# Transposes of v moved from DMA to TensorE, squared norms of k moved off it, gate bias preset in both tail banks, all ranks redrawn: a scheduled attention and highway kernel

## Chip, cores and metric

The kernel runs on one core of one Trainium2 chip. The metric is the device time of one execution in microseconds. A program on one core has no die to compare, so a run counts as fast unless it is over 1.5% above the fastest of its kernel. Ratios and their intervals are from fast runs alone. In the profile lines, PE is TensorE, PEld its weight loads, DVE VectorE, ACT ScalarE, POOL GpSimd and SP SyncE; L800 is line 800 of the kernel.

## The reference, cut to what matters

```python
# q, k, v: (4, 6336, 256) float32; tau = 1
qn = q / (np.linalg.norm(q, axis=1, keepdims=True) + 1e-06)    # norms over the 6336 rows
kn = k / (np.linalg.norm(k, axis=1, keepdims=True) + 1e-06)
s = kn.transpose(0, 2, 1) @ qn / tau                           # 256 x 256 for each batch
a = softmax(s)                                                 # over the last axis
x = (v @ a).reshape(-1, 256)                                   # 25344 x 256
H = np.maximum(x @ w_h, 0.0)
T = 1.0 / (1.0 + np.exp(-(x @ w_t + b_t)))
out = T * H + (1.0 - T) * x
```

## The kernel before

Each of the four batches has two stages. **Stage 1** runs over 50 subtiles of q and k (48 of 128 rows, two of 96) and adds up k'q, and beside it k'k and q'q, of which only the diagonals (the squared norms) are used. Then comes the **softmax chain**: norms, scaling, exp, and the folding of the two weight matrices into the attention matrix. **Stage 2** runs over 25 pairs of subtiles of v: v is transposed, and three products give h (before relu), t (before the gate) and x; ScalarE does relu and tanh, VectorE combines. Stage 1 of batch b+1 is woven into stage 2 of batch b. The 100 pairs are numbered through; "the tail" is what comes after pair TAIL, where stage 1 is over and its two PSUM banks serve h and t.

All of this goes through a planner: every piece of work is a task with an engine, a key (its rank: a smaller key goes first), durations, buffers that it takes and gives back. The planner simulates the engines and emits instructions in the order that it found. The constants at the top are ranks by kind of work, one number for each of batches 0, 1, 2 (from 2 on) and for the tail, and the order of loads.

```python
UNTIL = 73; AHEAD = 16; BY_DMA = 3; APART = 5; V_AHEAD = 2     # one line each in the file
PRIO = {
    ...
    "bias": (-28.394, 23.065, -1.772, 4.453),                  # batch 0, 1, 2, tail
    ...
}
HEAD = 5.5
TAIL = 66
ENDS = [18, 48.5, 62.25]        # pairs at which stage 1 of batches 1, 2, 3 is to be loaded

def stage1(b, s):               # cut
    for c in range(2):
        nc.tensor.matmul(sg[c][:, 0:C], kc, qa, start=first, stop=False)
        nc.tensor.matmul(sg[c][:, C : C + P], kc, kc, start=False, stop=False)
        if not apart(b, s // CH):            # b > 0 and chunk < APART: squares of q elsewhere
            nc.tensor.matmul(sg[c][:, C + P : C + 2 * P], qa[:, cs], qa[:, cs], ...)

def squares(b, j, half): ...    # ScalarE: Square of half a q chunk, 128 x 1024
def sum_squares(b, j, step): ...# GpSimd: adds them up to 128 x 256
def over_partitions(): ...      # TensorE: four small 32-bit matmuls against ones
# VectorE then adds that to the diagonal, and the softmax chain goes on

def transposes(b, i):           # TensorE; batch 3 as 16-bit, the others two halves as one 32-bit
def transpose_chunk(b, j):      # batch 3, chunks 3 to 6, by DMA on the queue of the stores
    nc.sync.dma_start(out=..., in_=src, transpose=True)

def preset(b, i):               # gate bias copied into the bank ahead of the products
    return t_tag(b, i) == "t"   # else a 512-column matmul row0 x btb puts it there
```

## Time and profile before

| | before |
|---|---|
| time, median of 4 runs | 269.76 us (269.4 to 270.33) |
| span of the profiled run | 268.3 us |
| first product of stage 2, last matmul, end | 45.65, 262.36, 268.35 us |
| TensorE work between these two, at full rate | 210.17 us |
| gaps of TensorE between these two | 6.65 us |

"Work" and "gaps" are used all through this text. Work is the sum over matmuls of the start-to-start distance at full rate (0.109 us for 256 columns and for a 32-bit transpose, 0.056 for 128, 0.216 for 512; the prediction shows how the timeline gives them). A gap is what lies between two starts beyond that. So the span is the first product (45.65) plus work plus gaps plus the end, less 0.11 us of the last matmul, which is in both the work and the end; the two sums are computed from the starts in the trace, and no matmul record is missing. Gaps before 90 us differ by up to about 1 us between runs with the same order there (1.5 to 2.3 us), so less than that is not read as an effect.

The groups of TensorE work that the change touches, in the list of groups by line and form; columns: line, engine, operation, tiles, shapes, count, then busy us and mean ns, then idle time before:

```profile
L453 PE MATMUL sg<-k 128*128 128x128 f16 x384 | 76.8, 223 | 0.0
L455 PE MATMUL sg<-q 128*128 128x128 f16 x144 | 32.5, 226 | 0.0
L760 PE MATMUL vtps<-ident,v 128*128 128x128 f32 x144 | 27.8, 275 | 0.9 <-DMA v<-in_v_dram 0.6 <-ACT vtsb L533 0.3
L754 PE MATMUL vtps<-ident,v 128*128 128x128 f16 x48 | 4.6, 219 | 0.0
L831 PE MATMUL t<-btb,row 128*128 128x512 f16 x16 | 6.1, 379 | 0.0
```

The counts matter here, not the busy times, in which pipelined matmuls overlap.

### The profile page before, as it was taken

Reading aid. Unit: us, or ns where it says so; the run is one execution under the profiler, and the core shown is the slowest. Engines: PE = TensorE matmul, PEld = TensorE weight load, DVE = VectorE, ACT = ScalarE, POOL = GpSimd, SP = SyncE. Lnnn points to the kernel's source line nnn. Section 1 sums busy time; section 2 is a strip of 40 time slices with the busy share of each in tenths; the row PEclk is TensorE's granted clock in tenths of the full one; section 3 lists DMA queues with packets and bytes.
Section 4 is the critical chain, followed back from the end, with each engine's and each line's share of the span. In section 5 each row is a group of like instructions: output and inputs, shape, how many; then the busy total and the mean of one; then the engine's idle time right before and its main releaser. Section 6 shows DMA issues by size and latency. Waiting matters only on the chain.

```text
span 268.3 us, 6249 instructions
## 1 busy us (share of the span) xinstructions
PE 246.4 (92%) x2430; PEld 216.6 (81%) x2430; DVE 181.6 (68%) x377; ACT 195.1 (73%) x365; POOL 131.7 (49%) x167
## 2 busy tenths in 40 slices
PE   0697977999999999999999999999999999999991
PEld 0596864889989978999999878999998778888880
DVE  1000035777766789557878797586878998998994
ACT  1001016978888789999898887787798999998980
POOL 7233468688778064695689138567655110000000
PEclk9999999999999999999999999999999999999998
DMA  6999999999999999999999999999999999999995
GB/s 107 215 211 208 206 206 202 212 213 214 214 213 212 213 214 255 247 263 269 275 286 258 267 267 254 249 236 281 287 280 239 284 214 304 379 399 165 351 423 232
DMA packets 24622, 67.24 MB, mean 251 GB/s; under 512 B 9104, under 2 KB 11280, under 8 KB 21648
## 3 DMA queue, kind: packets, MB, share of 16 engines
q0 software_dynamic: 13472, 39.20, 75.0%
q1 hardware_dynamic: 11120, 27.64, 29.0%
q8 instruction: 19, 0.31, 0.4%
q14 instruction: 11, 0.09, 0.1%
HBM read 78.38 MB, written 25.95 MB: 389 GB/s over the span
## 4 chain that ended last, share of the span: by engine, by line
PE 76%; DMA 12%; ACT 5%; POOL 2%; issue 2%; DVE 2%; ACTq 0%; DVEq 0%; POOLq 0%
PE h L800 16%; PE t L800 16%; PE d L800 15%; PE sg L452 12%; DMA k<-in_k_dram 10%; PE sg L453 6%; PE vtps L760 5%; DMA v<-in_v_dram 2%; ACT uu L854 2%; PE sg L455 2%; PE t L831 1%; PE vtps L754 1%; PE ah L689 1%; POOL q L327 1%; ACT d L840 1%
## 5 line engine op out<-in xcount | busy, mean ns | idle before, releaser
L800 PEld LDWEIGHTS <-vtsb 128*128 128x128 f16 (+1 forms) x1044 | 98.8, 99 | 17.3 <-issue 3.2
L452 PE MATMUL sg<-q,k 128*128 128x256 f16 x384 | 83.8, 277 | 12.7 <-DMA k<-in_k_dram 12.6
L861 DVE SCALAR_TENSOR_TENSOR pp<-uu,d 128x512 f32<-128x512 f32 (+1 forms) x100 | 68.0, 684 | 28.4 <-PE d L800 16.1
L453 PE MATMUL sg<-k 128*128 128x128 f16 x384 | 76.8, 223 | 0.0
L854 ACT ACTIVATE uu<-t 128x512 f32<-128x512 f32 (+1 forms) x100 | 59.7, 597 | 19.1 <-PE t L800 18.5
L880 DVE SCALAR_TENSOR_TENSOR o<-h,pp 128x512 f32<-128x512 f32 x96 | 65.5, 686 | 1.7
L840 ACT ACTIVATE d<-h 128x512 f32<-128x512 f32 (+1 forms) x100 | 57.9, 584 | 5.7 <-PE h L800 4.9
L800 PE MATMUL t<-mr,vtsb 128*128 128x256 f16 (+1 forms) x348 | 52.2, 272 | 1.5 <-ACT t L533 1.2
L800 PE MATMUL h<-mr,vtsb 128*128 128x256 f16 (+1 forms) x348 | 51.2, 272 | 0.5 <-ACT vtsb L533 0.5
L800 PE MATMUL d<-mr,vtsb 128*128 128x256 f16 (+1 forms) x348 | 51.5, 272 | 0.1
L452 PEld LDWEIGHTS <-k 128*128 128x128 f16 x384 | 38.0, 99 | 16.7 <-DMA k<-in_k_dram 13.9
L476 POOL TENSOR_TENSOR sq<-sq,sq 128x1024 f32<-128x1024 f32 x15 | 35.4, 2361 | 16.7 <-ACT sq L470 16.6
L453 PEld LDWEIGHTS <-k 128*128 128x128 f16 x384 | 38.0, 99 | 1.5
L533 ACT COPY t<-bias_all 128x512 f32<-128x512 f32 (+1 forms) x60 | 35.4, 591 | 1.4
L455 PE MATMUL sg<-q 128*128 128x128 f16 x144 | 32.5, 226 | 0.0
L470 ACT ACTIVATE sq<-q 128x1024 f32<-128x1024 f16 x30 | 31.3, 1053 | 0.0
L760 PE MATMUL vtps<-ident,v 128*128 128x128 f32 x144 | 27.8, 275 | 0.9 <-DMA v<-in_v_dram 0.6
L569 DVE SCALAR_TENSOR_TENSOR junk<-sg,ident 128x128 f32<-128x128 f32 x16 | 4.6, 288 | 33.2 <-PE sg L455 32.7
L535 DVE COPY vtsb<-vtps 128x256 f32<-128x256 f32 (+2 forms) x47 | 19.6, 418 | 7.0 <-PE vtps L760 6.7
L327 POOL DMA_DIRECT2D v<-in_v_dram x24 | 13.7, 571 | 18.9 <-PE vtps L760 11.7
L327 POOL DMA_DIRECT2D q<-in_q_dram x28 | 15.4, 552 | 15.1 <-DMA q<-in_q_dram 7.1
L327 POOL DMA_DIRECT2D k<-in_k_dram x28 | 15.3, 548 | 13.1 <-DMA k<-in_k_dram 9.2
(78 smaller groups left out, 249.5 us busy)
## 6 DMA issues: line engine op xcount, KB each, us to landing
out_dram<-o SPq DMA_DIRECT2D x23, 1024.0 KB, 9.6
v<-in_v_dram POOLq DMA_DIRECT2D x24, 512.0 KB, 16.6
q<-in_q_dram POOLq DMA_DIRECT2D x21, 512.0 KB, 16.2
k<-in_k_dram POOLq DMA_DIRECT2D x21, 512.0 KB, 18.0
q<-in_q_dram POOLq DMA_DIRECT2D x5, 256.0 KB, 9.6
k<-in_k_dram POOLq DMA_DIRECT2D x5, 256.0 KB, 8.9
out_dram<-o SPq DMA_DIRECT2D x2, 512.0 KB, 4.2
out_dram<-ot SPq DMA_DIRECT2D x4, 192.0 KB, 5.1
```

Source lines behind the costliest of these rows:

```text
L327: nc.gpsimd.dma_start(out=t[:, s : s + n, :], in_=main_rows(src)[:, j * CH + s : j * CH + s + n, :])
L452: nc.tensor.matmul(sg[c][:, 0:C], kc, qa, start=first, stop=False)
L453: nc.tensor.matmul(sg[c][:, C : C + P], kc, kc, start=False, stop=False)
L455: nc.tensor.matmul(sg[c][:, C + P : C + 2 * P], qa[:, cs], qa[:, cs], start=False, stop=last)
L476: add(out=sq, in0=sq, in1=other)
L533: nc.scalar.copy(out=out, in_=in_)
L760: nc.tensor.transpose(ps[:, u, 0:nr], v.bitcast(f32), ident0[0:nr, 0:nr])
L800: nc.tensor.matmul(out[0:nr, u, :], vt[u][kt][:, 0:nr], mr[kt][:, col * C : (col + 1) * C], **flags(u, kt))
L840: nc.scalar.activation(out=d[0:nr, :, :], in_=ps_t["h", b, i][0:nr, :, :], func=Act.Relu, scale=0.5)
L854: nc.scalar.activation(out=uu[0:nr, :, :], in_=ps_t.pop(("t", b, i))[0:nr, :, :], func=Act.Tanh, scale=-0.5)
L861: nc.vector.scalar_tensor_tensor(out=pp[0:nr, :, :], in0=el.pop(("uu", b, i))[0:nr, :, :], scalar=1.0, in1=ps_t.pop(("d", b, i))[0:nr, :, ...
L880: nc.vector.scalar_tensor_tensor(out=ot, in0=ps_t.pop(("h", b, i))[0:nr, :, :], scalar=0.0, in1=el.pop(("pp", b, i))[0:nr, :, :], op0=AluO ...
```

## The change

The intent is threefold: no DMA transposes (they slow other transfers), fewer matmuls for squared norms (two k chunks a batch, with one q chunk a batch given back), and fewer bias matmuls in the tail (ScalarE or VectorE copies the bias into either bank for three pairs in four). All ranks and the order of loads were drawn again.

```diff
-UNTIL = 73
-AHEAD = 16
-BY_DMA = 3
+UNTIL = 61
+AHEAD = -15                    # without effect: nothing is transposed by DMA
+BY_DMA = 7
-APART = 5
-V_AHEAD = 2
+APART = 4
+APART_K = 2
+V_AHEAD = 0.5
 PRIO = {
-    "bias": (-28.394, 23.065, -1.772, 4.453),
+    "bias": (-15.797, -52.319, -73.352, 56.321),
     ...                        # all other rows redrawn as well
 }
-HEAD = 5.5
-TAIL = 66
-ENDS = [18, 48.5, 62.25]
+HEAD = 8.5
+EVERY = 4
+TAIL = 64
+ENDS = [22.5, 42.25, 58.5]
...
-        return b == B - 1
+        return b == B - 1 and BY_DMA <= NJ          # natural(b): never now
...
-            nc.tensor.matmul(sg[c][:, C : C + P], kc, kc, start=False, stop=False)
-            if not apart(b, s // CH):
+            if not apart("k", b, s // CH):
+                nc.tensor.matmul(sg[c][:, C : C + P], kc, kc, start=False, stop=False)
+            if not apart("q", b, s // CH):
...                             # squares, sum_squares, plan_squares: for q and for k
-        return t_tag(b, i) == "t"
+        return t_tag(b, i) == "t" or (b * NP + i) % EVERY != 1
...
-                        lambda e, i=i: bias(b, i, e), take=["t"],
+                        lambda e, i=i: bias(b, i, e), take=[t_bank],
```

More of the change, by code (lines that the diff above doesn't have):

```diff
@@ L21 @@
 LAG = 5
-UNTIL = 73
-AHEAD = 16
-BY_DMA = 3
+UNTIL = 61
+AHEAD = -15
+BY_DMA = 7
 SHORT = 1.08
 MOVE = 165e3
-APART = 5
-V_AHEAD = 2
+APART = 4
+APART_K = 2
+V_AHEAD = 0.5
 PRIO = {
-    "tr": (24.974, 16.445, 34.195, 63.304),
-    "ev": (74.59, 73.008, 67.512, 50.704),
-    "h": (-53.39, -86.015, -64.208, -14.641),
-    "bias": (-28.394, 23.065, -1.772, 4.453),
-    "t": (4.111, -1.918, 67.766, 74.312),
-    "relu": (46.555, -20.175, -1.498, 14.915),
-    "x": (0.958, -19.433, 43.343, -6.4),
-    "gate": (-54.132, 37.28, -94.231, -112.222),
-    "prod": (-40.861, -10.819, -26.763, -55.482),
-    "res": (53.604, 18.42, 116.457, -9.113),
-    "s1": (117.419, 42.459, 84.45),
-    "sq": (-15.195, 72.384, 19.395),
+    "tr": (-41.544, -84.484, -71.287, -73.219),
+    "ev": (79.702, 164.382, 118.864, 152.575),
+    "h": (-104.744, -35.547, 40.328, 54.671),
+    "bias": (-15.797, -52.319, -73.352, 56.321),
+    "t": (-63.659, -149.979, -3.104, -73.919),
+    "relu": (-161.99, -110.892, 56.133, -126.746),
+    "x": (-150.758, -174.281, -305.464, -51.983),
+    "gate": (-109.784, -55.547, -191.652, -71.681),
+    "prod": (125.206, 114.192, 152.224, 33.14),
+    "res": (12.493, 105.005, -95.23, -167.161),
+    "s1": (78.544, 189.464, 249.341),
+    "sq": (-44.364, -12.223, -5.305),
 }
 POW = 0.75
-HEAD = 5.5
-TAIL = 66
+HEAD = 8.5
+EVERY = 4
+TAIL = 64
 EV = BIAS = ("ACT", "DVE")
-ENDS = [18, 48.5, 62.25]
+ENDS = [22.5, 42.25, 58.5]
 class Ring:
@@ L266 @@
         "q": QK_BUFS, "k": QK_BUFS, "v": V_BUFS, "tail_q": 2, "tail_k": 2, "tail_v": 2,
-        "sq": 2, "vT": 3, "vT_t": 1, "o": O_BUFS, "ot": 1, "uu": 3, "pp": 3, "vtsb": 9, "mr0": 2, "mr1": 2,
+        "sqq": 2, "sqk": 2, "vT": 3, "vT_t": 1, "o": O_BUFS, "ot": 1, "uu": 3, "pp": 3, "vtsb": 9, "mr0": 2, "mr1": 2,
         "sg0": 1, "sg1": 1, "vt": 1, "t": 1, "h": 2, "d": 2,
@@ L457, in stage1, with apart, squares, sum_squares @@
                 )
-    def apart(b, j):
-        return b > 0 and j < APART
+    def apart(nm, b, j):
+        return b > 0 and j < {"q": APART, "k": APART_K}[nm]
     sq_t = {}
     sums = {}
-    def squares(b, j, half):
-        sq_t[b, j, half] = sq = new("sq", [P, CH // 2, C], f32, f"sq{b}_{j}_{half}")
-        qa = tiles[("q", b, j)][:, half * CH // 2 : (half + 1) * CH // 2, :]
-        nc.scalar.activation(out=sq, in_=qa, func=Act.Square)
-    def sum_squares(b, j, step):
+    def squares(nm, b, j, half):
+        sq_t[nm, b, j, half] = sq = new("sq" + nm, [P, CH // 2, C], f32, f"sq{nm}{b}_{j}_{half}")
+        x = tiles[(nm, b, j)][:, half * CH // 2 : (half + 1) * CH // 2, :]
+        nc.scalar.activation(out=sq, in_=x, func=Act.Square)
+    def sum_squares(nm, b, j, step):
         add = partial(nc.gpsimd.tensor_tensor, op=AluOp.add)
         if step == 0:
-            sq, other = sq_t[b, j, 0], sq_t.pop((b, j, 1))
+            sq, other = sq_t[nm, b, j, 0], sq_t.pop((nm, b, j, 1))
             add(out=sq, in0=sq, in1=other)
         elif step == 1:
-            sq = sq_t[b, j, 0]
+            sq = sq_t[nm, b, j, 0]
             add(out=sq[:, 0:2, :], in0=sq[:, 0:2, :], in1=sq[:, 2:4, :])
         else:
-            sq = sq_t.pop((b, j, 0))
+            sq = sq_t.pop((nm, b, j, 0))
             if j == 0:
-                sums[b] = small.tile([P, C], f32, tag="sums", name=f"sums{b}")
-                add(out=sums[b], in0=sq[:, 0, :], in1=sq[:, 1, :])
+                sums[nm, b] = small.tile([P, C], f32, tag=f"sums{nm}", name=f"sums{nm}{b}")
+                add(out=sums[nm, b], in0=sq[:, 0, :], in1=sq[:, 1, :])
             else:
                 add(out=sq[:, 0, :], in0=sq[:, 0, :], in1=sq[:, 1, :])
-                add(out=sums[b], in0=sums[b], in1=sq[:, 0, :])
-    def plan_squares(b):
+                add(out=sums[nm, b], in0=sums[nm, b], in1=sq[:, 0, :])
+    def plan_squares(nm, b):
         ends, x = {}, None
-        for j in range(APART):
-            key = slot_of((b - 1) * NS + CH * j) + PRIO["sq"][b - 1]
+        for j in range({"q": APART, "k": APART_K}[nm]):
+            key = slot_of((b - 1) * NS + CH * j) + PRIO["sq"][b - 1] + (nm == "k")
             n0 = len(plan.tasks)
@@ L496, in plan_squares @@
                 plan.add(
-                    "ACT", key, 0.97, 1.07, loaded("q", b, CH * j + CH // 2 * n),
-                    lambda j=j, n=n: squares(b, j, n), take=["sq"],
+                    "ACT", key, 0.97, 1.07, loaded(nm, b, CH * j + CH // 2 * n),
+                    lambda j=j, n=n: squares(nm, b, j, n), take=["sq" + nm],
                 )
@@ L503, in plan_squares @@
             y = plan.add(
-                "POOL", key, 2.36, 2.45, parts, lambda j=j: sum_squares(b, j, 0), drop=[(parts[1], "sq")]
+                "POOL", key, 2.36, 2.45, parts, lambda j=j: sum_squares(nm, b, j, 0), drop=[(parts[1], "sq" + nm)]
             )
-            y = plan.add("POOL", key, 1.27, 1.35, [y], lambda j=j: sum_squares(b, j, 1))
+            y = plan.add("POOL", key, 1.27, 1.35, [y], lambda j=j: sum_squares(nm, b, j, 1))
             x = plan.add(
                 "POOL", key, 1.3 if j else 0.65, 1.4 if j else 0.75, [y] + ([x] if x else []),
-                lambda j=j: sum_squares(b, j, 2), drop=[(parts[0], "sq")],
+                lambda j=j: sum_squares(nm, b, j, 2), drop=[(parts[0], "sq" + nm)],
             )
@@ L513, in over_partitions @@
         def over_partitions():
-            sums[b, "ps"] = ps = new("vt", [P, 2], f32, f"sumps{b}")
+            sums[nm, b, "ps"] = ps = new("vt", [P, 2], f32, f"sumps{nm}{b}")
             for c in range(2):
-                nc.tensor.matmul(
-                    ps[:, c : c + 1], sums[b][:, bass.ts(c, P)], ones[:, 0:1], start=c == 0, stop=c == 1
-                )
+                x = sums[nm, b]
+                if nm == "q" or natural(b):
+                    x = x[:, bass.ts(c, P)]
+                else:
+                    x = x.rearrange("p (w two) -> p two w", two=2)[:, c, :]
+                nc.tensor.matmul(ps[:, c : c + 1], x, ones[:, 0:1], start=c == 0, stop=c == 1)
         def keep():
-            sums[b, "sb"] = sb = small.tile([P, 2], f32, tag="sumsb", name=f"sumsb{b}")
-            nc.vector.tensor_copy(out=sb, in_=sums[b, "ps"])
+            sums[nm, b, "sb"] = sb = small.tile([P, 2], f32, tag=f"sumsb{nm}", name=f"sumsb{nm}{b}")
+            nc.vector.tensor_copy(out=sb, in_=sums[nm, b, "ps"])
         p = plan.add("PE", key + 2, 0.4, 0.6, [x], over_partitions, take=["vt"])
@@ L535, in copy, with plan_chain @@
             nc.vector.tensor_copy(out=out, in_=in_)
-    def plan_chain(b, own, last, key, sums_of_q):
+    def plan_chain(b, own, last, key, apart_sums):
         st = {}
@@ L601, in dcat, with rest_of @@
                 )
-        def rest_of_q():
-            if sums_of_q:
-                xq = st["x"][:, 0:2]
-                nc.vector.tensor_tensor(out=xq, in0=xq, in1=sums[b, "sb"], op=AluOp.add)
+        def rest_of(nm, n):
+            if b:
+                x = st["x"][:, n : n + 2]
+                nc.vector.tensor_tensor(out=x, in0=x, in1=sums[nm, b, "sb"], op=AluOp.add)
         dq = dve(
-            lambda: (diagonal(0), diagonal(1), rest_of_q()), 0.9, 0.95, [last, consts] + sums_of_q
+            lambda: (diagonal(0), diagonal(1), rest_of("q", 0)), 0.9, 0.95, [last, consts] + apart_sums[:1]
         )
         nq = pool(lambda: norm(0), POW, POW + 0.2, [dq])
-        dk = dve(lambda: (diagonal(2), diagonal(3)), 0.75, 0.8, [dq])
+        dk = dve(
+            lambda: (diagonal(2), diagonal(3), rest_of("k", 2)), 0.9 if b else 0.75, 0.95 if b else 0.8,
+            [dq] + apart_sums[1:],
+        )
         nk = pool(lambda: norm(2), POW, POW + 0.2, [dk])
@@ L819, in preset @@
     def preset(b, i):
-        return t_tag(b, i) == "t"
+        return t_tag(b, i) == "t" or (b * NP + i) % EVERY != 1
     def bias(b, i, e):
         nr = rows(2 * i)
-        ps_t["t", b, i] = t = new("t", [P, 2, C], f32, f"t{b}_{i}")
+        ps_t["t", b, i] = t = new(t_tag(b, i), [P, 2, C], f32, f"t{b}_{i}")
         copy(e, t[0:nr, :, :], bias_all[0:nr, :, :])
@@ L937, in plan_stage1 @@
         x, own = None, []
-        part_ends, sums_of_q = ({}, []) if not apart(b, 0) else plan_squares(b)
+        part_ends, apart_sums = {"q": {}, "k": {}}, []
+        if b:
+            for nm in "qk":
+                part_ends[nm], z = plan_squares(nm, b)
+                apart_sums.append(z)
         for n, s in enumerate(order_of(b)):
@@ L941, in plan_stage1 @@
             deps = loaded("q", b, s) + loaded("k", b, s) + ([x] if x else [])
+            away = [nm for nm in "qk" if apart(nm, b, s // CH)]
             x = plan.add(
-                "PE", key, 0.33 if apart(b, s // CH) else 0.44, 0.66, deps, lambda s=s: stage1(b, s),
+                "PE", key, 0.44 - 0.11 * len(away), 0.66, deps, lambda s=s: stage1(b, s),
                 take=[sg_tag(b, n)] if n < 2 else [],
-                drop=([] if apart(b, s // CH) else drops("q", b, s)) + drops("k", b, s),
+                drop=[z for nm in "qk" if nm not in away for z in drops(nm, b, s)],
             )
             x.lat = x.pitch if n < NS - 1 else 0.66
-            if apart(b, s // CH) and s % CH == CH - 1:
-                plan.add("NONE", 0, 0, 0, [x] + part_ends[s // CH], None, drop=drops("q", b, s))
+            if s % CH == CH - 1:
+                for nm in away:
+                    plan.add("NONE", 0, 0, 0, [x] + part_ends[nm][s // CH], None, drop=drops(nm, b, s))
             if n < 2:
                 own.append((x, sg_tag(b, n)))
-        ready[b] = plan_chain(b, own, x, -50, [sums_of_q] if apart(b, 0) else [])
+        ready[b] = plan_chain(b, own, x, -50, apart_sums)
         if b == B - 1:
@@ L999, in plan_stage2 @@
                     plan.add(
-                        BIAS, pr("bias", g), (0.5, 0.6), (0.63, 0.72), [b_all] + before,
-                        lambda e, i=i: bias(b, i, e), take=["t"],
+                        BIAS, pr("bias", g), (0.5, 0.6), (0.63, 0.72), [b_all] + before + ends_of[t_bank],
+                        lambda e, i=i: bias(b, i, e), take=[t_bank],
                     )
```

## The prediction

> **What bounds the kernel now.** I read the page first (busy shares, slices, chain that ended last), then busy time by ten-microsecond stretch, then the timeline, because the pitch of instructions is only visible there.
>
> ```profile
> PE 246.4 (92%) x2430; PEld 216.6 (81%) x2430; DVE 181.6 (68%) x377; ACT 195.1 (73%) x365; POOL 131.7 (49%) x167
> PE   0697977999999999999999999999999999999991
> DMA  6999999999999999999999999999999999999995
> HBM read 78.38 MB, written 25.95 MB: 389 GB/s over the span
> PE 76%; DMA 12%; ACT 5%; POOL 2%; issue 2%; DVE 2%; ACTq 0%; DVEq 0%; POOLq 0%
> ```
>
> TensorE is busy in every slice from about 50 us on, and the chain of waits runs over TensorE for 76% of the span. But the DMA row is as full, so both are candidates. By stretch:
>
> ```profile
> 40.00:50.00 10.00, 8.19 (x67) 5.84 (x66) 6.18 (x15) 7.31 (x15) 8.62 (x11) 1.00 1.10 205
> 150.00:160.00 10.00, 9.07 (x91) 7.92 (x88) 8.48 (x30) 7.97 (x20) 3.01 (x5) 1.00 1.06 265
> 230.00:240.00 10.00, 9.99 (x100) 8.60 (x98) 9.54 (x16) 8.96 (x18) 0.00 (x0) 1.00 1.02 412
> 240.00:250.00 10.00, 10.00 (x92) 8.60 (x90) 9.20 (x16) 9.19 (x18) 0.00 (x0) 1.00 1.17 220
> ```
>
> Columns: stretch, length, then busy us of PE, weight load, VectorE, ScalarE, GpSimd, granted clock, DMA share, GB/s. In 240 to 250 us the DMA share is highest (1.17) while the rate falls from 412 to 220 GB/s: that is where v chunks of the last batch are transposed by DMA. TensorE does not go idle for it. VectorE and ScalarE are at 9.0 to 9.5 of 10 in the tail.
>
> "Busy" is not "at peak", so I took start-to-start distances from the timeline:
>
> ```profile
> 226.58 0.60 PE L800 MATMUL h<-mr,vtsb 128*128 128x256 f16 x4
> 227.01 0.60 PE L800 MATMUL d<-mr,vtsb 128*128 128x256 f16 x4
> 227.45 0.39 PE L754 MATMUL vtps<-ident,v 128*128 128x128 f16 x4
> 227.68 0.60 PE L800 MATMUL t<-mr,vtsb 128*128 128x256 f16 x4
> ...
> 248.71 0.38 PE L831 MATMUL t<-btb,row 128*128 128x512 f16 x1
> 248.93 0.27 PE L800 MATMUL t<-mr,vT 128*128 128x256 f16 x1
> ```
>
> Four 256-column products take 0.437 us (226.58 to 227.01 to 227.45), so 0.109 each; four 16-bit transposes 0.23; a 512-column bias matmul 0.22 (248.71 to 248.93). Two 32-bit transposes also take 0.22 (121.91 to 122.13 in the timeline). A whole subtile half of stage 1 (one 256- and two 128-column matmuls) repeats every 0.22 us (87.54 to 87.76), so a 128-column matmul is 0.055. Multiplying these by the counts of each line in each stretch gives work at full rate: 9.9 to 10.2 us in nearly every ten-microsecond stretch from 60 to 260. So TensorE really is the bound there. The exceptions are 50 to 60 (9.7), 90 to 100 (9.3), 150 to 160 (8.8) and 200 to 220 (19.1 of 20.4): the stretches where the softmax chain of the next batch runs. Gaps in all: about **5 us**. Stage 2 starts at 45.65 us; before that DMA bounds (batch 0's q and k must land, then the first v chunk, which lands at 44.6). After the last matmul (262.6) some 6 us of VectorE, store and landing remain.
>
> **What the Trainium skill says.** "TensorE: Matmul & The Clock Gate", section "Wait — 56ns, not 53.3ns?", gives start-to-start 55.6 ns for 128 columns and 215.7 ns for 512 once warm; the trace agrees (0.055 and 0.22 us), at a granted clock of 1.00. "Perfetto Trace Analysis", section "Identifying the Most-Contended Engine", warns that matmul busy time is no measure of distance to the roofline; hence the pitches above. "ScalarE: Activation LUTs", section "What ACT_TABLE_LOAD costs", says an ACTIVATE with immediates takes 186 ns + 0.833 ns per element and back-to-back ones overlap by about 93 ns. For 512 elements that is 613 and 520; the trace has 0.59 and 0.49 to 0.50:
>
> ```profile
> 225.47 0.59 ACT L854 ACTIVATE uu<-t 128x512 f32<-128x512 f32 x1
> 225.95 0.59 ACT L840 ACTIVATE d<-h 128x512 f32<-128x512 f32 x1
> 226.47 0.58 ACT L533 COPY t<-bias_all 128x512 f32<-128x512 f32 x1
> 226.97 0.60 ACT L854 ACTIVATE uu<-t 128x512 f32<-128x512 f32 x1
> ```
>
> So busy times of ScalarE are counted at 0.5 us per 512-wide instruction below. "Advanced Engine Details and Errata", section "X-Bar Transpose (TRN2)", calls transpose DMAs as fast as regular ones; the 220 against 412 GB/s above does not look like it.
>
> **The change part by part, on TensorE.**
> 1. No v transposed by DMA. Three chunks (12 pairs) and the short tail pair of the last batch, 13 pairs, now take two 32-bit transposes each: 13 x 0.22 = **+2.9 us**. The other 12 pairs of that batch swap four 16-bit for two 32-bit ones: 0.23 for 0.22, nothing.
> 2. k's squares of two chunks a batch leave TensorE: 3 batches x 16 subtiles x 2 = 96 matmuls x 0.055 = **-5.3**. But the eight subtiles of batch 1's first chunk run at 38.3 to 42.4 us, where TensorE is waiting anyway: 16 x 0.055 = 0.9 of that buys nothing.
> 3. The diff also lowers APART from 5 to 4: one q chunk a batch returns: 3 x 8 x 2 = 48 x 0.055 = **+2.6**.
> 4. k's sums over partitions need four more small matmuls a batch, 0.36 to 0.44 us before the next instruction (85.79 to 86.23, 204.94 to 205.30): 3 x 0.4 = **+1.2**.
> 5. Bias matmuls: odd pairs after pair 66 (17) become pairs with remainder 1 by four after pair 64 (65, 69, ... 97: 9): 8 x 0.22 = **-1.8**.
>
> Sum: 2.9 - 5.3 + 2.6 + 1.2 - 1.8 = -0.4; after 45.65 us, where it counts, -0.4 + 0.9 = **+0.5 us**. Thus the changed operations are nearly a trade of TensorE work against itself.
>
> **On the other engines.** ScalarE gains three net chunks of squares (2 x 3 x about 1.0 us = +6) and GpSimd about three adding-ups of 2.4 + 1.3 + 1.5 = 5.2 (+15). Bias presets rise by 8 (+4 to 5 us on either engine). v evictions become 25 narrow ones in place of 12 wide (25 x about 0.32 - 8 x 0.5 - 4 x 0.35 = +2.6). Body stretches have room. For the tail I count per pair: TensorE 3 x 0.437 + 0.22 + 0.22/4 = 1.59; ScalarE 2 x 0.5 + 0.29 eviction + 0.75 x 0.5 = 1.67 (0.29 is an estimate from 0.374 less the overlap), VectorE 2 x 0.61 = 1.22; shared evenly that is about 1.46 each. TensorE stays the bound, but with ScalarE and VectorE at 92%, which leaves little for bad order. Before, the DMA-transposed pairs took only 1.31 + 0.11 = 1.42 on TensorE.
>
> **On DMA.** The transposes go. At 220 instead of about 400 GB/s for ten microseconds they cost at least 4.5 us of DMA capacity; with the other two perhaps 6 to 10 (estimate). As TensorE did not wait for it, this by itself buys nothing. It makes room for the rest of the diff: q and k of the last batch are asked for some four pairs earlier (ENDS 62.25 to 58.5), stores are let loose at pair 61 rather than 73.
>
> **Retuned order.** All priorities are redrawn. What they can win is the 5 us of gaps around the chains and some idle time between 36.7 and 45.65 us; the latter hangs on landings that keep their order. I expect the tuner to have found about half of the gaps, -2.5 us, since someone kept this version. That is a choice, not a working.
>
> **Rivals.** (a) *Nothing is won*: the gaps stay, the +0.5 counts, and the time is 270 to 271. For it: gaps come from the chain itself, whose steps are unchanged. (b) *ScalarE and VectorE become the bound of the tail*: with a preset in each bank, each bank waits copy, products, tanh in a row (0.6 + 0.6 + 0.6 us), and with 92% load every hiccup shows. 33 pairs x 0.1 = 3 us more: 272 to 273. For it: tail stretches already at 9.0 to 9.5 of 10. Against: those count overlapping spans; at true pitch 8 to 10% is free. (c) *GpSimd delays loads*: four adding-ups in the first two chunks of a batch, about 20 us of in-order work, on the engine that issues loads. If a load is late, TensorE starves: +1 to 3 us. Against: 51% idle. (d) *DMA was the hidden limit*: total traffic 104.3 MB at the 420 GB/s of 10 to 40 us (210 GB/s counted on the 16-bit side, twice that read) is 248 us, plus start and transposes about 263, close to the span. If stores or late v throttle the pairs indirectly, removing 6 to 10 us lets TensorE close its gaps: 264 to 266. Against: no DMA wait of TensorE after 50 us among the longest waits.
>
> **Range and chances.** 269.9 + 0.5 - 2.5 = **267.9 us**. Rivals (a) to (c) reach 271.2 at moderate weight; (d) or a very good order reaches 265.2: range 265.2 to 271.2. Faster by over 2% needs under 264.5, i.e. all the gaps and more: 0.08. Slower by over 2% needs above 275.3, several rivals at once: 0.05. Within 2%: 0.87.
>
> **What would show it.** TensorE: 200-odd 32-bit transposes and none by DMA, 9 bias matmuls, 288 instead of 384 full k-square matmuls, 192 instead of 144 full q ones, work at full rate after 45 us within 1 us of before. DMA share near 240 us falls and GB/s no longer dips. Tail per pair near 1.59 us; if it is 1.7 or more with TensorE waiting for ScalarE or VectorE, (b) is right. Gaps near 95, 155 and 205 to 220 us should be about half. Wrong would be: a start of stage 2 well off 45.6 us, TensorE waiting for landings after 50 us, or a body that shortens by more than its work.

## More of the kernel before

The DMA part of the page:

```profile
DMA packets 24622, 67.24 MB, mean 251 GB/s; under 512 B 9104, under 2 KB 11280, under 8 KB 21648
q1 hardware_dynamic: 11120, 27.64, 29.0%
```

Queue q1 carries stores and DMA transposes.

## The result, and the profile after

| | before | after |
|---|---|---|
| time, median of 4 runs | 269.76 us | 271.17 us (270.89 to 271.3) |
| ratio | | 1.0041, 95% interval 1.0019 to 1.0062 |
| span of the profiled run | 268.35 | 269.04 |
| first product of stage 2 | 45.65 | 45.50 |
| work from there to the last matmul | 210.17 | 210.75 |
| gaps | 6.65 | 7.94 |
| of these before 90, 90 to 198, after 198 us | 1.6, 2.9, 2.1 | 1.5, 3.3, 3.2 |
| last matmul to end | 5.99 | 4.96 |

The change is slower by 0.4%: within 2%, but on the other side of zero than foretold. In the profiled runs, which lie 0.69 us apart: -0.15 (start) +0.58 (work) +1.29 (gaps) -1.03 (end) = +0.69.

The page after, the lines that answer to those of the prediction:

```profile
PE 246.1 (91%) x2388; PEld 216.8 (81%) x2388; DVE 191.7 (71%) x409; ACT 200.3 (74%) x366; POOL 143.9 (53%) x176
PE   0697977999999998999999899999999999999992
DMA  6999999999999999999999999999999999974435
HBM read 78.38 MB, written 25.95 MB: 388 GB/s over the span
PE 63%; DMA 20%; DVE 6%; POOL 4%; ACT 3%; issue 3%; DVEq 0%; POOLq 0%; ACTq 0%
```

The DMA row drops to 3 to 5 tenths in the last slices: the capacity is free. TensorE does not profit. That the chain has 20% DMA where it had 12% is no new bound: 8.6% of the span is one load, of the last rows of v of batch 1, which took 23.1 us, and TensorE waits 0.2 us for it. The groups of the changed work, by line and form, have the counts that were foretold (288 and 192 squares, 192 whole 32-bit transposes, 9 bias matmuls):

```profile
L456 PE MATMUL sg<-k 128*128 128x128 f16 x288 | 61.1, 224 | 0.0
L458 PE MATMUL sg<-q 128*128 128x128 f16 x192 | 42.9, 224 | 0.0
L770 PE MATMUL vtps<-ident,v 128*128 128x128 f32 x192 | 36.9, 274 | 0.7 <-DMA v<-in_v_dram 0.7
L841 PE MATMUL t<-btb,row 128*128 128x512 f16 x9 | 3.4, 379 | 0.0
```

And the DMA part of the page:

```profile
DMA packets 17869, 65.56 MB, mean 244 GB/s; under 512 B 2352, under 2 KB 4528, under 8 KB 14896
q1 hardware_dynamic: 4368, 25.96, 24.0%
```

Without the transposes there are 6752 fewer packets under 512 bytes. Stretches of ten microseconds after (columns as in the prediction):

```profile
150.00:160.00 10.00, 9.23 (x79) 7.62 (x76) 9.41 (x29) 8.42 (x20) 6.94 (x11) 1.00 1.06 276
210.00:220.00 10.00, 9.33 (x77) 7.48 (x76) 8.93 (x20) 8.97 (x20) 0.12 (x1) 1.00 1.03 327
230.00:240.00 10.00, 10.00 (x92) 8.90 (x91) 9.89 (x20) 9.23 (x18) 0.00 (x0) 1.00 0.93 312
240.00:250.00 10.00, 10.00 (x94) 9.02 (x92) 9.78 (x20) 9.55 (x19) 0.00 (x0) 1.00 0.53 215
```

VectorE is now at 9.8 to 9.9 in the tail, and still TensorE has no gaps there: between 225 and 262 us they sum to nothing (before: 0.7 us). The gaps stand where they stood, around the last two chains, and the one of the last batch is larger: 2.4 us between 198 and 225 us, where it was 1.4. The stretch of the kernel before that answers to the second line above:

```profile
210.00:220.00 10.00, 9.85 (x79) 7.67 (x77) 9.36 (x21) 9.48 (x23) 0.53 (x1) 1.00 1.07 247
```

Of the 2.4 us, 1.0 lies in two gaps at 215.2 and 216.3 us, where TensorE waits for ScalarE to write the folded matrix of the last batch; the kernel before has no such wait there.

The shorter end comes from the last store. The last VectorE result and the last issue before,

```profile
263.89 0.69 DVE L880 SCALAR_TENSOR_TENSOR ot<-h,pp 96x512 f32<-96x512 f32 x1
264.60 0.33 SPq L892 DMA_DIRECT2D out_dram<-ot  x1
```

and after:

```profile
265.25 0.69 DVE L890 SCALAR_TENSOR_TENSOR ot<-h,pp 96x512 f32<-96x512 f32 x1
265.96 0.33 SPq L902 DMA_DIRECT2D out_dram<-ot  x1
```

From issue to the end of the span it is 3.75 us before (268.35) and 3.08 after (269.04). The DMA engines are less busy by then (share 0.30 between 250 and 260 us, before 1.02); that this is what shortens it is not shown.

### The profile page after: what moved, and what is told of

It is laid out like the page before. It is cut to its first block, busy times and chain, and to the rows that moved or that the text cites. A ratio compares the mean times of both kernels' runs of the same rounds, so it can differ in the third digit from the quotient of the medians.

```text
span 269.0 us, 6180 instructions
## 1 busy us (share of the span) xinstructions
PE 246.1 (91%) x2388; PEld 216.8 (81%) x2388; DVE 191.7 (71%) x409; ACT 200.3 (74%) x366; POOL 143.9 (53%) x176
## 4 chain that ended last, share of the span: by engine, by line
PE 63%; DMA 20%; DVE 6%; POOL 4%; ACT 3%; issue 3%; DVEq 0%; POOLq 0%; ACTq 0%
PE h L810 13%; PE d L810 13%; PE t L810 13%; DMA k<-in_k_dram 10%; PE sg L454 9%; DMA v_t<-in_v_dram 9%; PE vtps L770 6%; PE sg L456 4%; DVE pp L871 2%; DMA v<-in_v_dram 2%; PE sg L458 2%; DVE o L890 2%; POOL q L329 1%; POOL k L329 1%; DVE vtsb L542 1%
## 5 line engine op out<-in xcount | busy, mean ns | idle before, releaser
L810 PEld LDWEIGHTS <-vtsb 128*128 128x128 f16 (+1 forms) x1200 | 114.6, 99 | 19.2 <-issue 5.2
L454 PE MATMUL sg<-q,k 128*128 128x256 f16 x384 | 80.3, 277 | 13.8 <-DMA k<-in_k_dram 12.9
L871 DVE SCALAR_TENSOR_TENSOR pp<-uu,d 128x512 f32<-128x512 f32 (+1 forms) x100 | 68.1, 682 | 19.2 <-PE d L810 14.9
L864 ACT ACTIVATE uu<-t 128x512 f32<-128x512 f32 (+1 forms) x100 | 59.5, 596 | 13.8 <-PE t L810 12.1
L456 PE MATMUL sg<-k 128*128 128x128 f16 x288 | 61.1, 224 | 0.0
L454 PEld LDWEIGHTS <-k 128*128 128x128 f16 x384 | 38.1, 100 | 18.1 <-DMA k<-in_k_dram 14.1
L458 PE MATMUL sg<-q 128*128 128x128 f16 x192 | 42.9, 224 | 0.0
L770 PE MATMUL vtps<-ident,v 128*128 128x128 f32 x192 | 36.9, 274 | 0.7 <-DMA v<-in_v_dram 0.7
L479 POOL TENSOR_TENSOR sqq<-sqq,sqq 128x1024 f32<-128x1024 f32 x12 | 28.4, 2369 | 8.7 <-ACT sqq L473 8.6
L542 DVE COPY vtsb<-vtps 128x256 f32<-128x256 f32 x70 | 29.2, 418 | 3.8 <-PE vtps L770 2.9
L456 PEld LDWEIGHTS <-k 128*128 128x128 f16 x288 | 28.7, 100 | 1.0
L770 PEld LDWEIGHTS vtps<-ident,v 128*128 128x128 f32 x192 | 23.4, 141 | 3.1 <-PE ah L699 1.1
L473 ACT ACTIVATE sqq<-q 128x1024 f32<-128x1024 f16 x24 | 25.0, 1052 | 0.0
L542 DVE COPY t<-bias_all 128x512 f32<-128x512 f32 x26 | 18.0, 692 | 9.1 <-ACT uu L864 8.9
```

Of the source, the lines that this page charges most:

```text
L479: add(out=sq, in0=sq, in1=other)
L542: nc.vector.tensor_copy(out=out, in_=in_)
L770: nc.tensor.transpose(ps[:, u, 0:nr], v.bitcast(f32), ident0[0:nr, 0:nr])
L810: nc.tensor.matmul(out[0:nr, u, :], vt[u][kt][:, 0:nr], mr[kt][:, col * C : (col + 1) * C], **flags(u, kt))
L864: nc.scalar.activation(out=uu[0:nr, :, :], in_=ps_t.pop(("t", b, i))[0:nr, :, :], func=Act.Tanh, scale=-0.5)
L871: nc.vector.scalar_tensor_tensor(out=pp[0:nr, :, :], in0=el.pop(("uu", b, i))[0:nr, :, :], scalar=1.0, in1=ps_t.pop(("d", b, i))[0:nr, :, ...
```

## The experiments

Twelve kernels ran, each beside the kernel before on the same chip (its medians there: 270.2 to 270.4 us), and all gave right results. All parts are planned, so a change of one constant can move thousands of instructions; some mixtures could not be planned at all ("no task can start": buffers held in a circle), and one raced. In old_parts_new_loads one of the six runs (299.42 us) is slow by the rule above and is not in the ratio; all other runs are fast. The table has the results; work, gaps and end are of the profiled runs.

| run | time us | ratio to before | work | gaps | of these after 198 us | end |
|---|---|---|---|---|---|---|
| before | 269.8 | 1 | 210.17 | 6.65 | 2.1 | 6.0 |
| after | 271.2 | 1.004 | 210.75 | 7.94 | 3.2 | 5.0 |
| old_no_dma_transpose | 272.8 | 1.008 | 212.94 | 6.56 | 1.8 | 5.4 |
| old_nodma_preset | 276.4 | 1.022 | 211.00 | 12.75 | 7.6 | 5.3 |
| nodma_preset_rank | 272.6 | 1.009 | 211.00 | 8.99 | 3.7 | 5.4 |
| old_k_squares | 275.2 | 1.018 | 209.70 | 11.52 | 4.0 | 6.3 |
| k_squares_rank | 279.8 | 1.034 | 209.70 | 16.04 | 7.6 | 6.6 |
| new_parts_old_order | 286.3 | 1.058 | 210.53 | 22.25 | 14.8 | 5.8 |
| old_parts_new_priorities | 278.3 | 1.029 | 210.17 | 13.78 | 8.5 | 6.9 |
| old_parts_new_loads | 295.2 | 1.088 | 210.17 | 31.38 | 25.7 | 6.2 |
| new_without_preset | 274.8 | 1.016 | 212.69 | 9.74 | 4.9 | 4.9 |
| new_with_dma_transpose | 275.7 | 1.021 | 209.92 | 11.44 | 6.5 | 7.0 |
| new_chain_first | 275.8 | 1.021 | 210.75 | 12.55 | 7.3 | 5.1 |
| new_retuned | 273.1 | 1.010 | 210.75 | 9.43 | 2.2 | 5.3 |

The theory to test: the three parts trade TensorE work against itself, with the sizes of the prediction, and the redrawn order won no gaps. The main rival: the parts by themselves open gaps, and the redrawn order had to mend them.

### Parts and order apart

New parts under the old order (the lead of v loads had to stay new for a plan to exist):

```diff
 # on the kernel after: UNTIL, PRIO, HEAD, TAIL, ENDS of the kernel before
-UNTIL = 61
+UNTIL = 73
-TAIL = 64
+TAIL = 66
 ...
```

> The three new mechanisms (no DMA transposes, k squares of two chunks off TensorE with q back at four chunks, bias presets for three pairs in four) under the old priorities, tail start, load order and store release; only the lead of v loads is the new 0.5 pairs. Theory 1 (the parts trade TensorE work against itself, +0.5 us, and the redrawn order won no gaps): within 1 us of before, 269 to 271. Theory 2 (the parts by themselves open gaps, and the new order had to mend them): 272 or more, with over 9 us of TensorE gaps after the first product. Theory 3 (the parts are good and the redrawn order spoils them): under 269.

286.34 us: theory 2, by far. Work is as it should be (210.53), gaps are 22.3 us, 14.8 of them after 198 us.

Old parts under the new ranks:

```diff
 # on the kernel before
-UNTIL = 73
+UNTIL = 61
-PRIO = { old }
+PRIO = { new }
```

> The kernel before with only the new priorities and the new store release (UNTIL 61). Theory 1: the priorities win nothing, 269.5 to 271.5, because several of the new keys rank ahead of the softmax chain and the gaps around the chain stay at 5 us or more. Theory 2 (the new order is the better one): under 268.5. Theory 3 (the new priorities cost): over 271.5.

278.27 us, 13.8 us of gaps: theory 3. So the new ranks are not better in themselves: moved to the other kernel's parts, either set of ranks opens gaps.

Old parts under the new order of loads:

```diff
 # on the kernel before
-UNTIL = 73
+UNTIL = 61
-V_AHEAD = 2
+V_AHEAD = 0.5
-HEAD = 5.5
+HEAD = 8.5
-ENDS = [18, 48.5, 62.25]
+ENDS = [22.5, 42.25, 58.5]
```

> The kernel before with only the new order of loads (HEAD, ENDS, V_AHEAD) and store release, old priorities, old mechanisms. Theory 1: TensorE is bound by its own work, so 269 to 271. Rival: earlier q and k of the last batch with DMA transposes still there starve v and stores: over 272.

295.21 us: the rival has the time right. Its mechanism is only a part. The waits from 225 us on, with their sum, times and longest, and three stretches:

```profile
PEld L800 <- DMA vT<-v: 8.1, 1, 8.1
PE t L800 <- DMA vT<-v: 7.7, 1, 7.7
PE h L800 <- DVE o L880: 7.8, 9, 1.1
```

```profile
235.00:245.00 10.00, 9.63 (x94) 8.16 (x91) 9.29 (x16) 8.54 (x18) 0.00 (x0) 1.00 1.30 64
245.00:255.00 10.00, 2.26 (x13) 1.37 (x12) 1.51 (x3) 1.02 (x2) 0.00 (x0) 0.68 1.20 139
255.00:265.00 10.00, 8.86 (x62) 6.83 (x61) 5.46 (x9) 5.92 (x11) 0.00 (x0) 0.81 1.04 257
```

TensorE stands still for 7.7 us until a chunk transposed by DMA lands; just before, the DMA engines are full (share 1.30) at only 64 GB/s. That is a third of the 25.7 us of gaps after 198 us. Some 2.6 us more are no waits: after the standstill the granted clock is lower (0.68 and 0.81 in these stretches) and 256-column matmuls start 0.21 us apart in place of 0.11, up to 258.8 us. Another 7.8 us are six gaps of 1.3 us between 262 and 283 us, where h waits for VectorE to give back its bank, not for a landing. That the earlier q and k are what makes the transposes late is not shown; the lead of v loads changed as well.

### The DMA transposes

```diff
 # on the kernel before
-BY_DMA = 3
+BY_DMA = 7
-        return b == B - 1
+        return b == B - 1 and BY_DMA <= NJ
```

> The kernel before with one constant changed, so that no v is transposed by DMA. Theory 1: 13 pairs x 0.22 us of transposes come on TensorE, and nothing comes back from DMA: before plus 2 to 3.5 us, 272 to 273.5, with 2.9 us more TensorE work. Rival (hidden DMA limit, rival d of the prediction): the 6 to 10 us of freed DMA capacity close gaps: 270.5 or less.

272.79 us, +0.8%: theory 1. Work rises by 2.77 us (foretold: 2.9), gaps stay (6.56), and only the end gets shorter, by 0.6 us. In the old order DMA was no hidden limit of TensorE.

The same in the new order, the other way round. This needed a kernel without presets in the second bank as its base (next section):

```diff
 # on new_without_preset (where AHEAD is 16 already, as in the kernel before)
-BY_DMA = 7
+BY_DMA = 3
```

> The changed kernel without presets in the second bank (274.8 us measured, 212.7 of work, 9.7 of gaps) and with the DMA transposes of the kernel before put back. Theory 1 (TensorE's work decides, DMA has room): work falls by 2.8 us and the time to 271 to 273. Rival (d') (the new order, which asks for v later and for q and k earlier, lives on the freed DMA time): gaps grow by what work falls, 274 or more.

275.68 us, against 274.83 without DMA transposes (other chip, same before within 0.1 us). Work falls by 2.77 us as it should, gaps rise by 1.7 and the end by 2.1. So the time is that of rival (d'): the new order does not get back the 2.8 us of work. That it lives on the freed DMA time is argued, not shown. GpSimd, which issues the loads, waits for a v buffer that a transpose still reads; its longest wait from 225 us on:

```profile
POOL v L329 <- DMA vT<-v: 16.4, 1, 16.4
```

But TensorE's own waits there are for ScalarE (five for the relu ahead of the x product, 2.0 us in all), and none for a landing. By the experiments above, any part that is exchanged under a fixed order can open gaps, and this run cannot tell the two apart.

### The presets

```diff
 # on the kernel after
-        return t_tag(b, i) == "t" or (b * NP + i) % EVERY != 1
+        return t_tag(b, i) == "t"
```

> The changed kernel with presets in the old bank alone, its order of work otherwise drawn from the same constants. Theory 1 (TensorE's work decides): 9 bias matmuls come back, 9 x 0.22 = 2.0 us more work, and the time is 2 to 3.5 us above the changed kernel, 273 to 275. Rival (b) of the prediction (ScalarE and VectorE bound the tail with the extra copies): taking away 9 copies gives time back, 271.5 or less.

274.83 us: work rises by 1.94 us (nine matmuls), gaps by 1.8. Taking the copies off ScalarE and VectorE gave no time back. The order was not redrawn for this, so the 1.8 us are no measure of the copies; against rival (b) of the prediction in the new order stands, more directly, that the kernel after has no gaps between 225 and 262 us.

In the old order, with the transposes on TensorE:

```diff
 # on old_no_dma_transpose
-        return t_tag(b, i) == "t"
+        return t_tag(b, i) == "t" or (b * NP + i) % EVERY != 1
```

> The kernel before without DMA transposes and with presets in both banks for three pairs in four, old order, old squares. Work: +2.9 - 9 x 0.22 (2.0) = +0.9 us. Theory A (it is the presets that the old order cannot carry, as seen in the slow run of all new parts): 274 to 279, TensorE gaps in the last 40 us of 3 us or more. Theory B (it is the squares that the old order cannot carry): 270 to 272.

276.40 us: work falls by 1.94 us, gaps rise by 6.2 us, nearly all after 198 us. The presets alone, under ranks drawn without them, cost 1.3% over old_no_dma_transpose. Is it the load of the copies, or their rank? One number tells:

```diff
 # on old_nodma_preset
-    "bias": (-28.394, 23.065, -1.772, 4.453),
+    "bias": (-28.394, 23.065, -1.772, 56.321),
```

> The kernel with no DMA transposes and presets for three pairs in four in the old order (276.4 us measured), with one number changed: the rank of the preset copies in the tail, from 4.453 to the 56.321 that the changed kernel uses, so that they come after other work of ScalarE and VectorE. Theory (the gaps that presets open are a matter of rank, not of load): gaps from the first product on fall from 12.8 to 9 us or less at the same 211.0 us of work, 272 to 273.5 us. Rival (the extra copies overload ScalarE and VectorE): 275 or more.

272.59 us: 3.8 us from one number, at the same work. Most of it is the rank: of the 6.2 us of gaps 3.8 close, and 2.4 more than in old_no_dma_transpose stay, whose cause is open. After 198 us TensorE waits eight times for ScalarE's relu ahead of the x product with the old rank (2.5 us in all), once with the new (0.7 us). A stretch of the tail with the old rank,

```profile
240.00:250.00 10.00, 9.31 (x80) 7.70 (x79) 9.63 (x19) 8.23 (x16) 0.00 (x0) 1.00 0.89 357
```

and with the new one:

```profile
240.00:250.00 10.00, 10.00 (x92) 8.91 (x90) 8.90 (x15) 9.34 (x21) 0.00 (x0) 1.00 1.00 413
```

TensorE starts 92 matmuls in place of 80; ScalarE does 21 instructions in place of 16 and VectorE 15 in place of 19, so more of the work that either can do lies with ScalarE. Over the whole tail (from 198 us) it is the evictions of transposed v that moved there, 25 in place of 14; of the bias copies it does 19 in place of 22.

### The squares

```diff
 # on the kernel before, with the code of the kernel after for the squares
-APART = 5
+APART = 4
+APART_K = 2
-V_AHEAD = 2
+V_AHEAD = 0.5                  # else no plan exists
```

> The kernel before with only the exchange of squares (two k chunks off TensorE, one q chunk back on it), old order but for the lead of v loads of 0.5 pairs that it needs to be feasible. Work -1.5 us in all, about -0.6 from the first product on. Theory B: 274 to 279, with the gaps in the batches' first halves, where GpSimd adds for two streams. Theory A: within 1.5 us of before.

275.24 us, so neither theory as written: both parts, the presets and the squares, are too much for the old order, while theory A had expected this one to be harmless and theory B the presets. Work falls by 0.47 us (foretold -0.6), gaps rise by 4.9. The shorter lead of v loads is in this run too, and no run has it alone (the kernel before with it has no plan), so the 4.9 us belong to the two together. One thing stands out in the timeline: the last matmul of batch 2's stage 1, the matmuls that add its q sums over partitions, and the first step of its chain.

```profile
147.49 0.22 PE L458 MATMUL sg<-q_t 96*128 96x128 f16 x1
...
154.42 0.50 PE L525 MATMUL sumpsq<-ones,sumsq 128*128 128x1 f32 x4
```

```profile
156.14 0.28 DVE L576 SCALAR_TENSOR_TENSOR junk<-sg,ident 128x128 f32<-128x128 f32 x1
```

The chain waits 8.6 us after stage 1 for a small sum of low rank. Mended by rank:

```diff
-        p = plan.add("PE", key + 2, 0.4, 0.6, [x], over_partitions, take=["vt"])
+        p = plan.add("PE", key + 2 - (60 if b == 2 else 0), 0.4, 0.6, [x], over_partitions, take=["vt"])
```

> The kernel before with the exchange of squares (275.2 us measured, 11.5 us of gaps), with the matmuls that add batch 2's sums over partitions ranked 60 places earlier. In the trace of the former run they came 7 us after the last matmul of that batch's stage 1, and the softmax chain began 8.6 us late. Theory (the gaps that the exchange opens come from this late sum): the chain of batch 2 begins within 2 us of its last stage-1 matmul, gaps between 145 and 198 us fall from 3.3 to 2 us or less and the total to 274 or less. Rival (the delay is hidden by pairs and what is won there is lost elsewhere, as the kernel's own planner has it with 276.7 in place of 272.6): 275 us or more.

The chain of batch 2 now begins 0.3 us after its stage 1, and the kernel takes 279.77 us with 16.0 us of gaps: the rival. The late sum was visible and was not what cost the time. What opens the gaps of this part in the old order is not settled.

### The chains and the order as a whole

```diff
 # on the kernel after
-        ready[b] = plan_chain(b, own, x, -50, apart_sums)
+        ready[b] = plan_chain(b, own, x, -500, apart_sums)
```

> The changed kernel with the softmax chain ranked ahead of everything (key -500 in place of -50; the new keys of relu, t, x and gate fall below -50, in the kernel before none that matter do). Theory (the gaps around the chains come from the chain being outranked): each chain gets 1 to 3 us shorter, gaps fall by 1 to 3 us, 268.5 to 270.5. Rival (the order of the pairs around the chain matters more than the chain's length; any change of rank costs): 272 to 276.

275.76 us: the rival. The chains of batches 1 and 2 are as long as before within 0.4 us (10.3, 12.6 against 10.3, 13.0 us from the last stage-1 matmul to the last folded matrix), that of batch 3 is 1 us longer (15.9 against 14.9), and gaps after 198 us rise from 3.2 to 7.3. Ranking the chain first does not close the gaps.

One number of the load order (ENDS, 58.5 to 61) was to show whether a later stage 1 fills the last chain:

> The changed kernel with one number of its load order changed: the last batch's q and k are spread up to pair 61 in place of 58.5 (the kernel before has 62.25). Theory (the gap of 2.4 us at 198 to 225 us is there because stage 1 ends at 201 instead of 206 us and leaves TensorE nothing to fill the last chain with): gaps at 198 to 225 us fall below 2 us and the time to 270 to 271. Rival (the order is drawn as a whole and hangs together; any single number moved costs several us elsewhere): 273 to 278.

With this order the plan writes an output buffer that a store still reads. That question stays open.

Last, the order of the changed kernel drawn once more, by 26,000 random steps on the planner's own estimate of its end:

```diff
 # on the kernel after: UNTIL, V_AHEAD, PRIO, HEAD, TAIL, ENDS
-ENDS = [22.5, 42.25, 58.5]
+ENDS = [23.0, 38.5, 57.5]
 ...
```

> The changed kernel with its priorities, load order, tail start and store release redrawn once more by a random search of 26,000 draws on the kernel's own planner (its estimate falls from 269.3 to 268.1; the same search over the kernel before found nothing under its 267.1). Theory 1 (the order, not the parts, is what the gaps come from, and the changed kernel's was less well drawn): 269.3 to 270.8, about 1 us under the changed kernel, by gaps and not by work. Rival (the planner's last microsecond does not carry to the chip): 271 or more.

273.08 us: the rival. The estimate fell by 1.2 us and the chip's time rose by 1.9. The planner's estimate is 2.7 us under the chip for the kernel before (267.1), 1.9 for the one after (269.3), 2.5 for new_parts_old_order (283.9), 4.4 for old_parts_new_priorities (273.9), 5.0 for this one and 14.6 for old_parts_new_loads (280.6). It has the sign of the change right (267.1 to 269.3), that of this redraw wrong, and it sorts disasters out; its last few microseconds are not the chip's. The same search over the kernel before gave nothing under its estimate.

## Why the prediction was wrong where it was

1. **What bounds the kernel: right.** The gaps, put at about 5 us, are 6.65 by the starts in the trace. The start of stage 2 is at 45.5 to 46.1 us and the work 209.7 to 212.9 us in all fourteen kernels; what sets their times apart by up to 25 us is the gaps.
2. **The work of the parts: right.** Foretold +0.5 us after 45.65 us; measured +0.58. Transposes 2.77 (2.9), squares -0.47 (-5.3 + 0.9 + 2.6 + 1.2 = -0.6), bias matmuls 8 x -0.216 = -1.7 (-1.8). Two small slips change nothing: the ScalarE starts shown lie 0.48 to 0.52 us apart, not 0.49 to 0.50, and 1.67 and 1.22 shared evenly is 1.44, not 1.46.
3. **The step that failed: "Retuned order ... about half of the gaps, -2.5 us, since someone kept this version."** The gaps rose by 1.3 us. The reasoning took the redrawn order as a gain on top of the parts. The runs show that neither order carries over to the other's parts. Under the old order the presets open 6.2 us of gaps (3.8 us of time come back with one rank), the squares with the shorter lead of v loads 4.9; all new parts under it have 22 us. The redrawn order brings this down to 7.9 us, a little above where the kernel before already was. That someone kept a version was no evidence on its time.
4. **Rival (a), nothing is won, 270 to 271: this is what came**, up to 0.2 us, and with a reason that it did not give: not only does the chain keep its gaps, the order also has new parts to fit. That the sum comes so close to (a) is partly luck: gaps (+1.29) and end (-1.03) nearly cancel, and neither was foretold.
5. **Rival (b), the bound moves to ScalarE and VectorE: wrong as a bound.** VectorE is at 9.8 to 9.9 of 10 in the tail, and TensorE has no gaps there; taking presets away gave no time back. But the same copies under another rank cost 3.8 us in the old order.
6. **Rival (c), GpSimd delays loads:** no run shows a load that came late through the adding-up; GpSimd's busy share rose from 49 to 53%. Not tested by itself.
7. **Rival (d), DMA as hidden limit: wrong for the old order** (gaps 6.65 and 6.56 with and without DMA transposes), and open for the new one, which gets slower with them (+1.7 us of gaps, +2.1 us at the end) without a wait of TensorE for a landing from 225 us on. Not foreseen was the shorter end: about 1 us, from 3.75 to 3.08 us for the last store and the rest from the order of the last pairs.
8. **Gaps "about half near 95, 155 and 205 to 220 us": wrong.** Between 198 and 225 us they went from 1.4 to 2.4. Two waits for the last folded matrix are 1.0 us of that. Why they came stays open: stage 1 of the last batch ends at 201.2 in place of 205.7 us, which leaves TensorE less to fill the last chain with, but the run that was to test this could not be made.

## What to carry to other kernels

When a change trades work of the bounding engine against itself, add up the trade first: it came out at +0.5 us here from counts and pitches, and the chip gave +0.58. Give a redrawn order no credit of its own: a tuned order fits the parts that it was drawn for, and a new part under it can open gaps of about ten times the work that it saves (the squares with the shorter lead of v loads: 4.9 against 0.47 us), while a single rank can be worth 3.8 us (the presets). If the kernel has a planner, ask it before forecasting (here it put the change at +2.2 us, measured +1.4), but do not believe differences of one or two microseconds: of the redraw it had the sign wrong.

## What the Trainium skill lacked or had wrong

- "Advanced Engine Details and Errata", section "X-Bar Transpose (TRN2)", calls transpose DMAs as fast as regular ones and expects 350 to 400 GB/s. Beside other traffic the rates here were far lower: with transposes in flight the stretch from 235 to 245 us of old_parts_new_loads has all 16 DMA engines full (share 1.30) at 64 GB/s, and the kernel before 220 GB/s at 240 us where it has 412 ten microseconds earlier. Its page counts 6752 more packets under 512 bytes than the kernel without transposes. In the packed trace of the kernel before, from 240 to 245 us, packets under 512 bytes (the transposes) move 0.52 MB and take 0.95 of the 16 engines' time, all others 0.46 MB and 0.23. These were 16-bit transposes from SBUF to SBUF in four issues; no run measures one alone, so the page's figure for that is not tested.
- "TensorE: Matmul & The Clock Gate" and "ScalarE: Activation LUTs" agreed with the traces, within 5%, in the sections that the prediction names (0.055 and 0.22 us for 128 and 512 columns; 0.59 us long and 0.48 to 0.52 us apart for 512 elements). What the first of them does not give is the start-to-start time of a 32-bit transpose of 128 columns: two take 0.22 us here, so 0.11 each, half the rate of a 16-bit one (four in 0.23 us).
- No page says how far a planned order carries over from one set of parts to another; the runs of exchanged parts, ranks or loads show 4.9 to 24.7 us of gaps opened that way (6.65 to 11.52 and to 31.38), at nearly the same work.
